# K blocks of six heads issued by ScalarE on its own DMA queue, in a decode step of two attention and two gated layers

## The chip, the cores and the metric

The kernel runs on one core of a Trainium2 chip. The metric is the device time of one execution in microseconds (us). The engines are named as in the profile: PE is TensorE (PEld its weight loads), DVE is VectorE, ACT is ScalarE, POOL is GpSimd and SP is SyncE. SPq and ACTq are the sequencers of SP and ACT, which issue DMA transfers. All transfers run on the 16 DMA engines of the core.

## The reference

One token for each of 4 batch rows goes through attention, a gated block, the same attention again (same weights, same caches) and the same gated block again, each with a residual:

```
x = x + A(layernorm(x));  x = x + B(layernorm(x));  x = x + A(layernorm(x));  x = x + B(layernorm(x))
A:  q = x @ wq                      # 32 query heads of 128, 8 key/value heads, 4 query heads share one
    k, v = the last 2048 of 8192 cached positions of each head
    out = softmax(q k^T / sqrt(128)) v @ wo
B:  (sigmoid(x @ w_gate) * (x @ w_up)) @ w_down      # width 512, inner width 1792
```

All is bf16 in memory. The cached K and V of one batch row and one key/value head are 2048 x 128, 512 KB; there are 32 such blocks of K and 32 of V, 16 MB each.

## The kernel before, in words

**Work and memory.** K of all 8 heads stays in SBUF in `kt` (32 blocks); K is loaded once, transposed in place, and used by both attention layers. V is loaded in both layers. In the first layer its blocks go to `arena`, 77 units of 256 columns, where a block takes 8 units; so 9 blocks fit, and `alloc` (L379) takes the space that was released longest ago. By that rule the second to fourth V block of head n take the place of V blocks of head n-2, the first that of the last block of head n-3. A load into such a place waits for the matmuls that read the old block. `wo` (8 parts of 512 KB in rows of 1 KB) is loaded head by head and stays.

**A head of the first layer**, in the loop at L809, n counting from 0:

- `k_head(n+1)` (L547): the 4 blocks of K of the next head are transposed on PE, 16 transposes a block (L559) in two halves through three PSUM banks, and copied back to `kt` by DVE (L566) and ACT (L570) in turn.
- `scores(n)` (L573): 16 matmuls of q with the transposed K (L583); the maximum on DVE (L592 to L602); the exponential `sexp` on ACT (L605), which writes `pbuf`, the token `("p",)` in the program; four matmuls that turn the probabilities (L614); a copy of them by ACT (L620, `ptc`); the sum and its reciprocal (L627 to L640).
- `load_wo(n)` and four loads of V, then `load_k(n+2)`.
- `pv_wo(n)` (L643): 64 matmuls with V (L656), 16 a block, a scaling on DVE (L666), and 16 matmuls with wo (L675).

All scores of this layer use one PSUM bank, so the scores of head n+1 wait for the exponential of head n.

**What sets the order.** The program lists its operations with what they read and write (`P.op`, L55). `_schedule` (L96) is a planner: it walks a model of the engines with the durations of a table (`_TM`, L259) and takes, on each engine, among the operations that could start within 60 ns of the earliest, the one that is first in the program. This fixes the order on PE, DVE and ACT. DMA transfers are all on SP, apart from the small load of x on ACT (L465), and SP keeps the order of the program: K0, wq, K1, wo0, V0, K2, wo1, V1, K3 and so on (the digit is the head). In the model the transfers go one behind the other through one pipe (L160 to L163). `_assign_sync` (L186) then gives each operation a semaphore and its waits; a DMA on SP gets one of 32 semaphores in turn. An operation given in `order=` comes ahead on the same engine, without a wait on a semaphore.

K of the seventh and eighth head goes to places in `kt` that hold wq at the start (L801 to L806), so those loads also wait for the q projection, which is long over by then.

**Behind the first layer** come the residual, the gated block (`glu`, L708; its weights go to the arena in places that V of the seventh and eighth head leave free), the q projection of the second layer, its V blocks, and the second gated block.

Of the kernel before, what the change touches and what calls it, by code (L numbers as in the profile page):

```python
# [95 lines left out]
def _schedule(ops, tm):  # L96
    for o in ops:
        o.users = []
    for o in ops:
        o.ndeps_left = len(o.deps) + len(o.odeps)  # L100
        for d in o.deps:
            d.users.append(o)
        for d in o.odeps:
            d.users.append(o)
    ready = dict((e, []) for e in ENGINES)
    order = dict((e, []) for e in ENGINES)
    eng_free = dict((e, 0.0) for e in ENGINES)
    sync_all = sorted((o for o in ops if o.eng == "sync"), key=lambda o: (o.prio, o.idx))
    sync_ptr = 0
    for o in ops:  # L110
        if o.ndeps_left == 0:
            ready[o.eng].append(o)
    pipe_free = 0.0
    outstanding = []
    nleft = len(ops)
    tol = tm["pick_tol"]
    sem_lat = tm["sem_lat"]
    while nleft:
        best = None
        best_key = None  # L120
        for e in ENGINES:
            if e == "sync":
                if sync_ptr >= len(sync_all) or sync_all[sync_ptr].ndeps_left:
                    continue
                cand = (sync_all[sync_ptr],)
            else:
                cand = ready[e]
                if not cand:
                    continue
            ef = eng_free[e]  # L130
            tmin = None
            ests = []
            for o in cand:
                t = ef
                for d in o.deps:
                    td = d.finish + sem_lat
                    if td > t:
                        t = td
                ests.append((t, o))
                if tmin is None or t < tmin:  # L140
                    tmin = t
            pick = None
            for x in ests:
                if x[0] <= tmin + tol and (pick is None or x[1].prio < pick[1].prio):
                    pick = x
            key = (pick[0], pick[1].prio)
            if best is None or key < best_key:
                best = pick
                best_key = key
        if best is None:  # L150
            raise RuntimeError("scheduler deadlock")
        t0, o = best
        e = o.eng
        if e == "sync":
            sync_ptr += 1
            if o.dma_bytes:
                if len(outstanding) >= tm["dma_max_out"]:
                    outstanding.sort()
                    t0 = max(t0, outstanding[-tm["dma_max_out"]])
                issue_end = t0 + tm["dma_issue"]  # L160
                xs = max(pipe_free, issue_end + tm["dma_lat0"])
                xe = xs + o.dma_bytes / o.dma_rate
                pipe_free = xe  # L163
                o.start = t0
                o.finish = xe + tm["dma_lat1"]
                outstanding.append(o.finish)
                eng_free[e] = issue_end
            else:
                o.start = t0
                o.finish = t0 + o.dur  # L170
                eng_free[e] = o.finish
        else:
            o.start = t0
            o.finish = t0 + o.dur
            eng_free[e] = o.finish
            ready[e].remove(o)
        order[e].append(o)
        nleft -= 1
        for u in o.users:
            u.ndeps_left -= 1  # L180
            if u.ndeps_left == 0 and u.eng != "sync":
                ready[u.eng].append(u)
    return order


def _assign_sync(ops, order, n_dma_sems):  # L186
    counts = {}
    dma_i = 0
    for e in ENGINES:
        for o in order[e]:  # L190
            if o.sem is not None:
                sem = o.sem
            elif e == "sync":
                sem = ("dma", dma_i % n_dma_sems)
                dma_i += 1
                o.inc = 16
            else:
                sem = ("eng", e)
                o.inc = 1
            o.sem = sem  # L200
            counts[sem] = counts.get(sem, 0) + o.inc
            o.val = counts[sem]
    prev_user = {}
    for o in order["sync"]:
        p = prev_user.get(o.sem)
        if p is not None:
            o.deps.add(p)
        prev_user[o.sem] = o
    snap = {}
    known = dict((e, {}) for e in ENGINES)  # L210
    pos = dict((e, 0) for e in ENGINES)
    done = set()
    total = sum(len(order[e]) for e in ENGINES)
    ndone = 0
    while ndone < total:
        progressed = False
        for e in ENGINES:
            oe = order[e]
            kn = known[e]
            while pos[e] < len(oe):  # L220
                o = oe[pos[e]]
                ok = True
                for d in o.deps:
                    if d.idx not in done:
                        ok = False
                        break
                if not ok:
                    break
                need = {}
                for d in o.deps:  # L230
                    if need.get(d.sem, 0) < d.val:
                        need[d.sem] = d.val
                waits = []
                for s in sorted(need, key=str):
                    v = need[s]
                    if kn.get(s, 0) >= v:
                        continue
                    waits.append((s, v))
                    kn[s] = v
                    ps = snap.get((s, v))  # L240
                    if ps is not None:
                        for s2, v2 in ps.items():
                            if kn.get(s2, 0) < v2:
                                kn[s2] = v2
                o.waits = tuple(waits)
                sn = dict(kn)
                if sn.get(o.sem, 0) < o.val:
                    sn[o.sem] = o.val
                snap[(o.sem, o.val)] = sn
                done.add(o.idx)  # L250
                pos[e] += 1
                ndone += 1
                progressed = True
        if not progressed:
            raise RuntimeError("sync assignment deadlock")
    return counts
# [12 lines left out]
def build(nc, A_x, A_k, A_v, A_wq, A_wo, B_wg, B_wu, B_wd, out):  # L269
    tm = dict(_TM)  # L270
# [40 lines left out]
    def kv_d(cache, b, h):  # L311
        return cache[b, h, SK - W:SK, :].rearrange("(p j) d -> p (j d)", p=128)

    es = contextlib.ExitStack()
    with es:
# [38 lines left out]
        x_sem = es.enter_context(nc.semaphore("x_in"))  # L354
        eng_sems = dict((e, es.enter_context(nc.semaphore("s_" + e))) for e in ENGINES if e != "sync")
        dma_sems = [es.enter_context(nc.semaphore("s_dma%d" % i)) for i in range(N_DMA_SEMS)]

        P = _Plan()

# [50 lines left out]
        def c_act(n):  # L410
            return tm["act_fix"] + n * tm["act_el"]

        def dma(name, dst, src, w, r=(), rate="bw_4k", nbytes=None, sem=None):
            if nbytes is None:
                nbytes = dst.partition_size() * dst.free_nbytes()
            o = P.op("sync", name, 0.0, lambda e, dst=dst, src=src: e.dma_start(dst, src),  # L416
                     r=r, w=w, dma_bytes=nbytes, dma_rate=tm[rate])
            if sem is not None:
                o.sem = sem
                o.inc = 16  # L420
            return o

        def load_block(name, cache, b, h, s):
            dma(name, blk_ap(s), kv_d(cache, b, h), w=blk_tok(s))


        P.op("gpsimd", "ones", 200.0, lambda g: g.memset(ones_f[:], 1.0), w=[("ones_f",)])
# [359 lines left out]
        TBK = [(0, "vector"), (1, "scalar"), (2, "vector"), (0, "scalar"), (1, "vector"), (2, "scalar")]  # L787
        layer_norm(0, math.log(SCALE))

        def load_k(h):  # L790
            for b in range(NB):
                load_block("K_%d_%d" % (h, b), A_k, b, h, kblk(h, b))

        def load_wo(h):
            dma("wo_%d" % h, wo_sb[:, h * WOH:(h + 1) * WOH].rearrange("p (r n) -> p r n", r=REP),
# [13 lines left out]
        for n, h in enumerate(HEADS1):  # L809
            if n + 1 < HKV:  # L810
                k_head(HEADS1[n + 1], TBK)
            scores(0, n, h, 3, MB)
            load_wo(h)
            vs = []
            for b in range(NB):
                s = alloc()
                load_block("V0_%d_%d" % (h, b), A_v, b, h, s)
                vs.append(s)
            if n + 2 < HKV:
                load_k(HEADS1[n + 2])  # L820
            pv_wo(0, n, h, (5, 6), vs)
            for b in range(NB):
                release(vs[b])
# [49 lines left out]
        def sem_h(s):  # L873
            if s[0] == "eng":
                return eng_sems[s[1]]
            if s[0] == "dma":
                return dma_sems[s[1]]
            return x_sem if s[0] == "xin" else out_sem

        def run_engine(eng, name):  # L880
# [49 lines left out]
```

## Time and profile before

| what | value |
|---|---|
| three runs | 190.92, 191.29 and 204.33 us, median 191.29 |
| the profiled execution | 191.58 us, of which the span from first to last instruction is 189.7 us |
| busy | PE 136.0 us (72%), PEld 113.5 (60%), DVE 65.1 (34%), ACT 53.7 (28%), POOL 2.1 (1%) |
| mean granted TensorE clock | 0.684 |
| DMA | 72.48 MB, mean 382 GB/s; 72.10 MB of it on the queue of SP |
| transposes of K on PE (L559) | 47.1 us, 512 of them |
| matmuls with V from the arena (L656) | 23.0 us, idle before them 13.9, of which 13.8 to V's DMA |
| the exponential (L605) | 687 ns each, 16 of them |
| first layer's last V matmuls end | 110.2 us from the start of the span |

Shares are of the span. In the slices of the page, each of the 40 digits stands for 4.74 us and gives tenths of busy time. In lines of the order of time, the columns are the start, the duration, the engine and line, the operation, what it writes and reads, how many were merged, and in brackets the idle time of the engine just before with what ended it. An issue of a transfer is a line of SPq or ACTq; its duration is the issue alone, and the data land later. Idle time of an engine that is not the bottleneck costs nothing.

### The profile page before, as it was taken

What the parts mean: (1) busy time and instruction counts of PE and PEld (TensorE: products, weight loads), DVE (VectorE), ACT (ScalarE), POOL (GpSimd) and SP (SyncE); (2) the same over time, 40 slices, a digit from 0 to 9 for tenths busy, and PEclk for the clock granted to TensorE, in tenths of its full rate; (3) what the DMA queues carried; (4) which work ended last, traced back from release to release, by engine and by line L of the source; (5) the groups of instructions that cost most, each with busy time, mean ns of one, the idle gap of its engine ahead of it and who ended that gap; (6) DMA issues with size and microseconds to landing.
All of it is one profiled execution on the core that took longest, in us unless ns stands there. A gap on an engine that the chain in (4) does not pass through costs nothing.

```text
span 189.7 us, 6050 instructions
## 1 busy us (share of the span) xinstructions
PE 136.0 (72%) x2760; PEld 113.5 (60%) x2760; DVE 65.1 (34%) x204; ACT 53.7 (28%) x91; POOL 2.1 (1%) x10
## 2 busy tenths in 40 slices
PE   2944886979869598795786465364669799985574
PEld 2933764968759397593784354363327466674463
DVE  4410255436345343454244020220067163530220
ACT  2440162554626336263172000000043122220010
POOL 4000000000000000000000000000000000000000
PEclk9996589588797957969579555555597555555555
DMA  6999999999999999999999999999999999999980
GB/s 220 380 416 418 400 403 409 388 411 396 401 406 388 409 399 399 408 390 408 398 397 394 404 406 382 370 355 375 415 413 410 407 407 405 411 409 404 387 272 15
DMA packets 25281, 72.48 MB, mean 382 GB/s; under 512 B 2212, under 2 KB 9896, under 8 KB 24744
## 3 DMA queue, kind: packets, MB, share of 16 engines
q1 hardware_dynamic: 25248, 72.10, 98.2%
q8 instruction: 21, 0.34, 0.7%
q14 instruction: 4, 0.03, 0.0%
q10 hardware_dynamic: 8, 0.00, 0.0%
HBM read 72.09 MB, written 0.00 MB: 380 GB/s over the span
## 4 chain that ended last, share of the span: by engine, by line
DMA 63%; PE 23%; DVE 5%; SPq 4%; ACT 2%; issue 2%; ACTq 0%; DVEq 0%
DMA arena<-in_A_v_cache_dram 33%; DMA kt<-in_A_v_cache_dram 9%; DMA kt<-in_A_k_cache_dram 8%; PE ps L559 6%; DMA arena<-in_B_w_gate_dram 6%; PE ps L583 5%; SPq L416 4%; PE ps L656 4%; DMA arena<-in_B_w_down_dram 4%; DMA arena<-in_A_wq_dram 4%; PE ps L720 2%; ACT pbuf L605 2%; PE ps L675 1%; PE ps L760 1%; PE ps L484 1%
## 5 line engine op out<-in xcount | busy, mean ns | idle before, releaser
L559 PE MATMUL ps<-ident_b,kt 128*128 128x128 bf16 x512 | 47.1, 278 | 0.6 <-DMA kt<-in_A_k_cache_dram 0.3
L559 PEld LDWEIGHTS ps<-ident_b,kt 128*128 128x128 bf16 x512 | 44.9, 131 | 1.3 <-DMA kt<-in_A_k_cache_dram 0.8
L570 ACT COPY kt<-ps 128x1024 bf16<-128x1024 bf16 x32 | 32.2, 1012 | 34.2 <-PE ps L559 33.4
L656 PE MATMUL ps<-pt,arena 128*128 128x4 bf16 x704 | 23.0, 165 | 13.9 <-DMA arena<-in_A_v_cache_dram 13.8
L566 DVE COPY kt<-ps 128x1024 bf16<-128x1024 bf16 x32 | 22.1, 692 | 28.2 <-PE ps L559 28.2
L656 PEld LDWEIGHTS ps<-pt,arena 128*128 128x128 bf16 x704 | 20.4, 99 | 17.8 <-DMA arena<-in_A_v_cache_dram 17.4
L605 ACT ACTIVATE pbuf<-ps,nmg 128x512 bf16<-128x512 f32 x16 | 11.0, 687 | 43.8 <-DVE nmg L602 33.4
L583 PE MATMUL ps<-kt,qs 128*32 128x512 bf16 x256 | 21.2, 466 | 1.8 <-ACT kt L570 1.3
L592 DVE TENSOR_REDUCE nm<-ps 128x1 f32<-128x512 f32 x16 | 10.9, 682 | 17.1 <-PE ps L583 17.1
L656 PE MATMUL ps<-pt,kt 128*128 128x4 bf16 x320 | 10.3, 166 | 4.5 <-issue 3.3
L656 PEld LDWEIGHTS ps<-pt,kt 128*128 128x128 bf16 x320 | 9.5, 104 | 5.3 <-issue 4.0
L583 PEld LDWEIGHTS ps<-kt,qs 128*32 128x32 bf16 x256 | 6.2, 109 | 8.4 <-issue 3.7
L675 PE MATMUL ps<-onb,wo_sb 128*128 128x4 bf16 x256 | 9.2, 167 | 2.8 <-DVE onb L666 2.4
L675 PEld LDWEIGHTS ps<-onb,wo_sb 128*128 128x128 bf16 x256 | 8.3, 104 | 4.1 <-issue 2.6
L620 ACT CAST pt<-ps 128x256 bf16<-128x256 f32 x16 | 6.0, 372 | 14.9 <-PE ps L614 14.9
L666 DVE TENSOR_TENSOR onb<-ps,rz 128x16 bf16<-128x16 f32 x16 | 3.1, 194 | 17.6 <-PE ps L656 17.4
L509 ACT ACTIVATE lnl<-ps 128x4 f32<-128x4 f32 x4 | 0.7, 176 | 29.2 <-PE ps L484 29.2
L614 PEld LDWEIGHTS ps<-ident_b,pbuf 128*128 128x128 bf16 x64 | 3.3, 108 | 8.8 <-ACT pbuf L605 5.7
L614 PE MATMUL ps<-ident_b,pbuf 128*128 128x64 bf16 x64 | 5.4, 215 | 4.2 <-ACT pbuf L605 4.2
L523 PE MATMUL ps<-xn,kt 128*128 128x4 bf16 x128 | 3.9, 166 | 6.1 <-DMA kt<-in_A_wq_dram 6.1
L720 PE MATMUL ps<-xn,arena 128*128 128x4 bf16 x168 | 5.7, 167 | 3.5 <-DMA arena<-in_B_w_up_dram 1.2
L523 PE MATMUL ps<-xn,arena 128*128 128x4 bf16 x128 | 4.7, 167 | 4.9 <-DMA arena<-in_A_wq_dram 4.3
(60 smaller groups left out, 79.2 us busy)
## 6 DMA issues: line engine op xcount, KB each, us to landing
arena<-in_A_v_cache_dram SPq DMA_DIRECT2D x44, 512.0 KB, 12.6
kt<-in_A_k_cache_dram SPq DMA_DIRECT2D x32, 512.0 KB, 13.0
kt<-in_A_v_cache_dram SPq DMA_DIRECT2D x20, 512.0 KB, 13.8
kt<-in_A_wq_dram SPq DMA_DIRECT2D x4, 1024.0 KB, 11.6
wo_sb<-in_A_wo_dram SPq DMA_DIRECT2D x8, 512.0 KB, 14.8
arena<-in_A_wq_dram SPq DMA_DIRECT2D x8, 512.0 KB, 7.0
arena<-in_B_w_gate_dram SPq DMA_DIRECT2D x4, 448.0 KB, 10.5
arena<-in_B_w_up_dram SPq DMA_DIRECT2D x4, 448.0 KB, 10.8
```

The source lines that it names most:

```text
L416: o = P.op("sync", name, 0.0, lambda e, dst=dst, src=src: e.dma_start(dst, src), r=r, w=w, dma_bytes=nbytes, dma_rate=tm[rate])
L523: last = pe.matmul(ps[:, QB, q * NB:(q + 1) * NB], ap[:, (q - q0) * 128:(q - q0 + 1) * 128], xn[:, ktc * NB:(ktc + 1) * NB], start=(st and ...
L559: last = pe.transpose(bankb(bank)[:, jj * 128:(jj + 1) * 128], half[:, jj * 128:(jj + 1) * 128], ident_b[:, :])
L566: lambda v, half=half, bank=bank: v.tensor_copy(half, bankb(bank)[:, 0:1024]),
L570: lambda a, half=half, bank=bank: a.copy(half, bankb(bank)[:, 0:1024]),
L583: last = pe.matmul(ps[32 * b:32 * b + 32, sbk, 0:CB * 128], qs[:, q0:q0 + 32], blk_ap(kblk(h, b))[:, c * CB * 128:(c + 1) * CB * 128], sta ...
L592: lambda v: v.tensor_reduce(nmv, ps[:, sbk, 0:CB * 128], AXX, ALU.max, negate=True),
L605: lambda a: a.activation(pbuf[:, :], ps[:, sbk, 0:CB * 128], ACTF.Exp, bias=gv, scale=1.0, accum_out=zv),
L614: last = pe.matmul(to[:, k], pbuf[:, k * 128:(k + 1) * 128], sel, start=True, stop=True, skip_group_check=True)
L656: last = pe.matmul(ps[:, obk, b * REP:(b + 1) * REP], blk_ap(s)[:, (c * CB + k) * 128:(c * CB + k + 1) * 128], pt[:, w0:w0 + REP], start=( ...
L675: last = pe.matmul(ps[:, WB, c * NB:(c + 1) * NB], wo_sb[:, h * WOH + r_ * D + c * 128: h * WOH + r_ * D + (c + 1) * 128], ov[:, r_ * NB:( ...
L720: last = pe.matmul(ps[:, bank, fc * NB:(fc + 1) * NB], blk_ap(s)[:, fc * 128:(fc + 1) * 128], xn[:, ktc * NB:(ktc + 1) * NB], start=(ktc = ...
```

## The change

`load_k` for the third to eighth head (`n + 2` in the loop, so 24 blocks of 512 KB) is given to ACT's DMA queue in place of SP's. Each head's four issues are ordered behind the last writer of `pbuf` at that place of the program, which is the exponential of head n, two heads in front. This is an order on ACT, not a wait on a semaphore. K of the first two heads stays on SP.

The planner is taught of DMA on other engines: such an issue takes ACT for the table's issue time (450 ns), its data go through the same modelled pipe, and they are not counted in the limit of 16 outstanding transfers that SP has in the model. The second queue gets 32 semaphores of its own.

```
...                                 # _schedule, between the cases of sync and of the compute engines
+        elif o.dma_bytes:
+            issue_end = t0 + tm["dma_issue"]
+            xe = max(pipe_free, issue_end + tm["dma_lat0"]) + o.dma_bytes / o.dma_rate
+            pipe_free = xe
+            o.start = t0
+            o.finish = xe + tm["dma_lat1"]
+            eng_free[e] = issue_end
+            ready[e].remove(o)
...
-            elif e == "sync":
-                sem = ("dma", dma_i % n_dma_sems)
-                dma_i += 1
+            elif o.dma_bytes:
+                sem = ("dma" if e == "sync" else "dmaq", dma_i[e] % n_dma_sems)
+                dma_i[e] += 1
                 o.inc = 16
...
-        def dma(name, dst, src, w, r=(), rate="bw_4k", nbytes=None, sem=None):
+        def dma(name, dst, src, w, r=(), rate="bw_4k", nbytes=None, sem=None, eng="sync", order=()):
...
-            o = P.op("sync", name, 0.0, lambda e, dst=dst, src=src: e.dma_start(dst, src),
-                     r=r, w=w, dma_bytes=nbytes, dma_rate=tm[rate])
+            o = P.op(eng, name, 0.0, lambda e, dst=dst, src=src: e.dma_start(dst, src),
+                     r=r, w=w, dma_bytes=nbytes, dma_rate=tm[rate], order=order)
...
-        def load_k(h):
+        def load_k(h, **kw):
             for b in range(NB):
-                load_block("K_%d_%d" % (h, b), A_k, b, h, kblk(h, b))
+                load_block("K_%d_%d" % (h, b), A_k, b, h, kblk(h, b), **kw)
...
             if n + 2 < HKV:
-                load_k(HEADS1[n + 2])
+                load_k(HEADS1[n + 2], eng="scalar", order=[P.last_w[("p",)]])
             pv_wo(0, n, h, (5, 6), vs)
```

More of the change, by code (lines that the diff above doesn't have):

```diff
@@ L187, in _assign_sync @@
     counts = {}
-    dma_i = 0
+    dma_i = dict((e, 0) for e in ENGINES)
     for e in ENGINES:
@@ L203, in _assign_sync @@
     prev_user = {}
-    for o in order["sync"]:
+    for o in [o for e in ENGINES for o in order[e] if o.dma_bytes]:
         p = prev_user.get(o.sem)
@@ L356, in build @@
         dma_sems = [es.enter_context(nc.semaphore("s_dma%d" % i)) for i in range(N_DMA_SEMS)]
+        dmaq_sems = [es.enter_context(nc.semaphore("s_dmaq%d" % i)) for i in range(N_DMA_SEMS)]
         P = _Plan()
@@ L421, in dma, with load_block @@
             return o
-        def load_block(name, cache, b, h, s):
-            dma(name, blk_ap(s), kv_d(cache, b, h), w=blk_tok(s))
+        def load_block(name, cache, b, h, s, **kw):
+            dma(name, blk_ap(s), kv_d(cache, b, h), w=blk_tok(s), **kw)
         P.op("gpsimd", "ones", 200.0, lambda g: g.memset(ones_f[:], 1.0), w=[("ones_f",)])
@@ L877, in sem_h @@
                 return dma_sems[s[1]]
+            if s[0] == "dmaq":
+                return dmaq_sems[s[1]]
             return x_sem if s[0] == "xin" else out_sem
```

## The prediction

> **What bounds the kernel now.** I read the slices of the span first, then the chain that ended last, then the stretches of the eight heads with their DMA share, and last the order of time on SP, ACT and PE. The slices and the chain, from the profile's page:
>
> ```profile
> DMA  6999999999999999999999999999999999999980
> GB/s 220 380 416 418 400 403 409 388 411 396 401 406 388 409 399 399 408 390 408 398 397 394 404 406 382 370 355 375 415 413 410 407 407 405 411 409 404 387 272 15
> ...
> DMA 63%; PE 23%; DVE 5%; SPq 4%; ACT 2%; issue 2%; ACTq 0%; DVEq 0%
> ...
> arena<-in_A_v_cache_dram SPq DMA_DIRECT2D x44, 512.0 KB, 12.6
> kt<-in_A_k_cache_dram SPq DMA_DIRECT2D x32, 512.0 KB, 13.0
> ```
>
> All 16 DMA engines are at 90% or more from the second slice to the last but two, and the chain is mostly DMA. A K block lands a median 13.0 us after its issue, though 0.524 MB at 401 GB/s last 1.3 us: some ten transfers are always queued. Two stretches of the first attention layer, columns PE, PEld, DVE, ACT and POOL busy, granted clock, DMA share, GB/s:
>
> ```profile
> 52.00:64.00 12.00, 9.52 (x174) 8.05 (x166) 4.89 (x12) 5.20 (x7) 0.00 (x0) 0.86 1.03 400
> 64.00:76.00 12.00, 10.07 (x170) 9.14 (x166) 4.92 (x12) 5.20 (x7) 0.00 (x0) 0.72 1.04 401
> ```
>
> The DMA share is 1.03 and over (packets overlap a little), so the engines never rest. A head moves 9 transfers (4 K, 4 V, one wo), 4.72 MB, which at 401 GB/s take **11.8 us**; that is the period of the heads. PE is busy 9.5 to 10.1 of 12 us, so it is close behind. A change of who issues the transfers moves the end only if it leaves the DMA engines without work, or makes a head's chain of compute longer than 11.8 us.
>
> **The change part by part.** The issues on SP and the exponentials on ACT, in order of time:
>
> ```profile
> 19.15 3.94 SPq L416 DMA_DIRECT2D kt<-in_A_k_cache_dram  x4
> 32.46 2.26 SPq L416 DMA_DIRECT2D kt<-in_A_k_cache_dram  x4
> 55.51 2.51 SPq L416 DMA_DIRECT2D kt<-in_A_k_cache_dram  x4
> ...
> 29.39 0.69 ACT L605 ACTIVATE pbuf<-ps,nmg 128x512 bf16<-128x512 f32 x1 [1.50 <-DVE nmg L602]
> 33.31 0.69 ACT L605 ACTIVATE pbuf<-ps,nmg 128x512 bf16<-128x512 f32 x1 [2.39 <-PE ps L656]
> 54.01 0.69 ACT L605 ACTIVATE pbuf<-ps,nmg 128x512 bf16<-128x512 f32 x1 [2.69 <-PE ps L656]
> ```
>
> *Removed from SP*: 24 issues at a median 434 ns, 10.4 us of a queue that mostly stands with its ring full (the first V issue, at 8.20 us, lasted 8.15 us). Worth nothing by itself. SP then runs ahead with wo and V until the arena's slots stop it (V of head n, second block on, needs the slots of head n-2).
>
> *Added to ACT*: 4 issues a head, from 0.434 us (SP's row) to 0.56 us (ACT's one issue, x, at 0.81 us): 1.7 to 2.2 us behind each of six exponentials. I take 1.8. Behind them on ACT wait the copy of the transposed probabilities (L620), for which PV waits, and the copies of the next transposes (L570). In the fourth head the exponential ends at 54.78 us and the first such copy starts at 57.75: 2.97 us, less 0.37 for L620, is 2.6 us of cover. Cost **0**; without the cover it would be 1.8 us a head, 11 us in all.
>
> *Moved in time*: if the exponentials stayed where they are, the third head's K would be issued at 30.2 instead of 19.15 us, the fourth's at 34.1 instead of 32.46, the sixth's at 54.8 instead of 55.51, and the others within 0.7 us of now. So only the third head's K is really late, by 11 us. How long K then takes no row shows, since nothing now shares the engines with a second queue. Bounds: 2.10 MB alone at 401 GB/s, 5.2 us; the slowest transfer of now, 19.2 us from issue to landing. I take 10 to 13 us, next to the row of 13.0.
>
> The Trainium skill, "DMA: Bandwidth & Descriptors", section "Queues, rings and completion order", says that each DMA engine takes turns between its queues packet by packet; K would then have half the rate, an estimate of 10.5 us for four blocks, inside what I take. No trace of before shows it. Its section "Issuing engines are not separate DMA queues" speaks against the change: issuing from several engines saves only issue time. The 10.4 us above, off the critical path, agree.
>
> So the third head's K is there at 42 to 45 us, its transposes end at 44 to 46 instead of 40.0, and everything behind them is **4 to 6 us late**. Is that kept, lost or repaid? A head as PE runs it now:
>
> ```profile
> 55.12 0.28 PE L614 MATMUL ps<-ident_b,pbuf 128*128 128x64 bf16 x4
> 55.64 0.54 PE L675 MATMUL ps<-onb,wo_sb 128*128 128x4 bf16 x16 [0.24 <-DVE onb L666]
> 56.04 5.62 PE L559 MATMUL ps<-ident_b,kt 128*128 128x128 bf16 x64
> 61.50 0.20 PE L635 MATMUL ps<-zd,ones_b 128*128 128x16 bf16 x2
> 62.59 0.55 PE L656 MATMUL ps<-pt,arena 128*128 128x4 bf16 x16 [0.90 <-DMA arena<-in_A_v_cache_dram]
> 63.08 1.05 PE L583 MATMUL ps<-kt,qs 128*32 128x512 bf16 x16
> ```
>
> The planner takes, of what is ready within 60 ns, the operation that is earliest in the program, and it believes that K queues behind all that SP has issued. Working its rule by hand (for the order, not for a time), I get per head: transposes of n+1, PV of n whole, scores of n+1, softmax, transposes of n+2. Now PV straddles the scores. The chain of a head would be 5.62 (transposes) + 1.74 (PV, the row at 42.12 us) + 1.05 (scores) + 1.57 (end of scores at 64.13 to exponential at 65.70) + 0.78 (exponential) + 0.28 (L614) = **11.0 us**, against 11.8 us of DMA. The lateness shrinks by some 0.7 us a head and is 2 to 4 us at the last. K of head n+2 is wanted, last block, about 16 us behind the exponential of n (11 + 0.4 + 4.2), so 10 to 13 us are in time. The engines starve only if V's slots and K both run out; SP has by the slots always 6 to 8 us of transfers issued ahead. The end of the layer now:
>
> ```profile
> 103.59 0.28 PE L614 MATMUL ps<-ident_b,pbuf 128*128 128x64 bf16 x4
> ...
> 109.57 0.59 PE L656 MATMUL ps<-pt,arena 128*128 128x4 bf16 x16 [0.67 <-DMA arena<-in_A_v_cache_dram]
> ```
>
> The last head's probabilities are copied at 104.27 us and its last V block comes at 109.5; the three blocks before need 1.3 us, so softmax may be 3.9 us late for nothing. What is over falls on the gated block, whose matmuls wait for weights from 115.35 to 118.81 us: another 3 us. With 2 to 4 us late, I charge **0.4 us** for the two places where the engines could run short (the K wait of the third head, the first weight issue at 102.35 us, which waits for PV of the seventh head).
>
> **Sum**: SP 0, ACT 0, lateness 0.4. The profiled execution took 191.58 us (span 189.7, 1.9 around it), 0.3 above the median of the three runs, 191.29. Forecast **192.0 us**, its own range 190.3 to 194.2. A measurement of this kernel tells about 2% (3.8 us) from no change.
>
> **The rivals.**
> 1. *K comes last and the lead of two heads is lost (slower).* Now K of a head lands two heads before its V. If the ACT queue's K lands over 16 us behind its exponential, because SP's backlog of V goes first, every head waits for K, and the eighth head's K lands with the last V. Then behind the last landing stand transposes of a block (1.4), its copy (1.1), scores 1.05, softmax 2.35, L614 0.28, copy 0.45 and PV 1.74 = 8.4 us, where now one block's 0.6 stands; less the 3 us that the gated block absorbs, +4.8: **196.4 us** (194 to 198). For it: 19.2 us occurs now. Against: K's own queue is then short. 21%.
> 2. *ACT stands in the issue.* SP's K issues reach 2.45 us when the ring is full. If ACT's last 1.3 us each (the pace of landing), 5.2 us a head stand before the copies against 2.6 of cover: 2.6 x 6 heads = 15.6, less 3.9 and 3 of slack: +8.7, **200.3 us**. Against: ACT has at most 8 blocks out, and SP got 13 transfers out before its ring stopped it. 9%.
> 3. *Two queues move more bytes.* If the rate of the heads (401) rose to that of the slices at 10 to 19 us (417), the 80 us from 30 to 110 shrink by 3.1: **188.5 us**, 1.6% faster. Against: the lower rate goes with wo's short rows, which stay. 8%, half of it over 2%.
> 4. *The order is all that the change sets*: the issues may be planned behind other ACT work, later than the exponential. By 2 to 6 us, this leads into rival 1 and is counted there.
>
> **How the numbers follow.** Forecast 60%, rival 1 21%, rival 2 9%, rival 3 8%, an unnamed loss 2%. Slower by over 2% (above 195.4): most of rival 1 (17), rival 2 (9), 3 of the forecast, 2 unnamed = 31%. Faster by over 2%: 5%. Within: 64%. The range from 188.8 to 198.0 holds the forecast, most of rival 1 and half of rival 3, and leaves out rival 2.
>
> **What would show it.** Right: DMA share 1.0 and about 400 GB/s in every stretch from 10 to 110 us; ACT's issues near 0.45 us each; exponentials of heads four to eight 2 to 6 us later than now; last V block at 109 to 111 us; transposes from the fifth head on not waiting for K. Rival 1: idle time of the transposes put down to K's DMA, and PV without waits for V. Rival 2: ACT issues above 1 us and copies waiting behind them. Rival 3: over 410 GB/s in the heads. What makes me wrong most easily: the order that the planner writes, which I have only by hand, and the share of the engines that the second queue gets.

## The result, and the profile after

The changed kernel takes 192.68 us (median of 20 runs, 191.07 to 194.79) against 191.42 us of the kernel before (20 runs): a ratio of **1.0053, 95% interval 1.0033 to 1.0073**, 1.0 us slower. The ratio leaves out slow runs, those over 1.5% above the fastest of their kernel (one of 20 on either side), so it isn't quite that of the two medians. The forecast was 192.0 us with no change clear of 2%, and its range holds the time. In the experiments below, on two different chips, the same kernel came to 1.0012 (0.9978 to 1.0046) and 1.0040 (1.0009 to 1.0071).

The page of the changed kernel, its slices and its chain:

```profile
DMA  5999999999999999999999999999999999999980
GB/s 206 425 427 411 393 402 390 403 399 402 405 389 403 396 404 400 398 409 393 406 402 393 354 363 399 365 405 411 407 408 411 406 408 403 412 407 405 391 285 16
...
PE 44%; DMA 25%; SPq 13%; DVE 8%; ACT 6%; issue 3%; ACTq 0%; DVEq 0%
...
arena<-in_A_v_cache_dram SPq DMA_DIRECT2D x44, 512.0 KB, 15.5
kt<-in_A_k_cache_dram ACTq DMA_DIRECT2D x24, 512.0 KB, 10.6
```

Two stretches of the heads, and the one where the first layer ends:

```profile
52.00:64.00 12.00, 8.49 (x166) 7.58 (x166) 4.93 (x13) 5.10 (x7) 0.00 (x0) 0.86 1.04 397
64.00:76.00 12.00, 8.41 (x166) 7.46 (x166) 6.16 (x16) 5.20 (x7) 0.00 (x0) 0.85 1.03 400
100.00:110.00 10.00, 7.99 (x156) 7.08 (x154) 4.66 (x12) 4.80 (x7) 0.00 (x0) 0.84 0.99 373
```

The rate in the heads is what it was (397 and 400 GB/s, before 400 and 401), and K on ACT's queue lands a median 10.6 us behind its issue. But the chain has changed hands: mostly PE where it was mostly DMA. The stretch from 100 to 110 us moved 399 GB/s before and moves 373 now. The mean granted clock, 0.664 against 0.684, is not what makes the difference: beside e9 the kernel before took 190.8 to 191.5 us in executions at 0.663 and 190.9 to 191.7 us at 0.685.

This profiled execution, 191.07 us, is the fastest of the 20, so it shows the mechanism but not the whole loss. A second look at the same kernel (e9 below, span 191.7 us, 2.0 us over the profile of before) has the same shape with a larger hole.

Where the time begins to be lost, in the order of time on PE from the second to the fourth head, changed kernel:

```profile
34.91 0.57 PE L665 MATMUL ps<-pt,arena 128*128 128x4 bf16 x16
37.10 0.59 PE L665 MATMUL ps<-pt,arena 128*128 128x4 bf16 x16 [1.63 <-DMA arena<-in_A_v_cache_dram]
39.67 0.59 PE L665 MATMUL ps<-pt,arena 128*128 128x4 bf16 x16 [1.97 <-DMA arena<-in_A_v_cache_dram]
42.22 0.58 PE L665 MATMUL ps<-pt,arena 128*128 128x4 bf16 x16 [1.96 <-DMA arena<-in_A_v_cache_dram]
43.18 0.57 PE L684 MATMUL ps<-onb,wo_sb 128*128 128x4 bf16 x16 [0.38 <-DVE onb L675]
43.61 6.05 PE L568 MATMUL ps<-ident_b,kt 128*128 128x128 bf16 x64
50.78 1.05 PE L592 MATMUL ps<-kt,qs 128*32 128x512 bf16 x16 [1.12 <-ACT kt L579]
```

The same stretch in the kernel before (L559 are the transposes, L656 PV):

```profile
33.14 1.01 PE L559 MATMUL ps<-ident_b,kt 128*128 128x128 bf16 x8
...
34.42 5.55 PE L559 MATMUL ps<-ident_b,kt 128*128 128x128 bf16 x56
...
42.12 1.74 PE L656 MATMUL ps<-pt,arena 128*128 128x4 bf16 x64
```

In the changed kernel the four blocks of V of the second head (L665) arrive 2.56 us apart, 205 of the 402 GB/s, beside K of the third and fourth head on the other queue. The transposes of the third head (L568) stand behind them in PE's order and start at 43.6 us; in the kernel before they stood in front of that PV and started at 33.1.

Starts of the eight exponentials of the first layer, from the order of time on ACT (us):

| kernel | 1 | 2 | 3 | 4 | 5 | 6 | 7 | 8 |
|---|---|---|---|---|---|---|---|---|
| before | 29.4 | 33.3 | 44.0 | 54.0 | 65.7 | 77.9 | 89.2 | 102.3 |
| changed | 29.2 | 33.1 | 53.4 | 65.5 | 76.2 | 87.7 | 98.2 | 108.8 |
| late by | -0.2 | -0.2 | 9.5 | 11.5 | 10.5 | 9.8 | 9.0 | 6.5 |

From the fourth to the eighth head the changed kernel takes 10.8 us a head, the kernel before 12.1. It catches up 5 of 11.5 us, not all. What is left meets the first gate weight, which waits for PV of the seventh head to leave its place. The queue of SP, first the changed kernel, then its second look (e9):

```profile
105.86 0.33 SPq L425 DMA_DIRECT2D arena<-in_B_w_gate_dram  x1
```

```profile
108.18 0.33 SPq L425 DMA_DIRECT2D arena<-in_B_w_gate_dram  x1
```

Before, this issue came at 102.35 us. SP's last V issue ends at 96.3 us (changed) and 98.1 us (e9), SP then issues nothing for ten us, and the engines run dry. In stretches, the kernel before and then e9:

```profile
100.00:110.00 10.00, 5.26 (x150) 4.13 (x138) 2.25 (x8) 1.15 (x3) 0.00 (x0) 0.70 1.04 399
110.00:118.00 8.00, 4.95 (x125) 4.48 (x122) 1.15 (x7) 0.38 (x2) 0.00 (x0) 0.50 1.04 395
```

```profile
100.00:110.00 10.00, 8.57 (x166) 7.83 (x166) 4.45 (x12) 5.10 (x7) 0.00 (x0) 0.83 0.84 314
110.00:118.00 8.00, 4.30 (x107) 3.96 (x107) 2.79 (x14) 1.15 (x3) 0.00 (x0) 0.67 0.97 358
```

At 399 GB/s the missing bytes of e9 are worth 10 x (399 - 314)/399 = 2.1 us and 8 x (395 - 358)/395 = 0.7 us. A part comes back: from 126 to 135 us e9 moves 409 GB/s and the kernel before only 374, 0.8 us. The net, 2.0 us, is the difference of the two spans. In the fastest execution the same sums are 0.7 + 0.2 - 0.7, and it ends even with before. Both kernels move the same bytes, so such a sum tells where the time goes, not why.

### The profile page after: what moved, and what is told of

Read it like the earlier page. It is cut to its first block, busy times and chain, and to the rows that moved or that the text cites. A ratio compares the mean times of both kernels' runs of the same rounds, so it can differ in the third digit from the quotient of the medians.

```text
span 189.3 us, 6057 instructions
## 1 busy us (share of the span) xinstructions
PE 133.5 (70%) x2760; PEld 110.5 (58%) x2760; DVE 65.7 (35%) x204; ACT 53.5 (28%) x91; POOL 2.1 (1%) x10
## 4 chain that ended last, share of the span: by engine, by line
PE 44%; DMA 25%; SPq 13%; DVE 8%; ACT 6%; issue 3%; ACTq 0%; DVEq 0%
PE ps L568 17%; SPq L425 13%; DMA kt<-in_A_v_cache_dram 9%; DMA arena<-in_A_v_cache_dram 9%; PE ps L592 8%; PE ps L665 8%; DMA arena<-in_A_wq_dram 4%; DMA arena<-in_B_w_down_dram 3%; PE ps L729 3%; ACT pbuf L614 3%; DVE nm L601 3%; ACT kt L579 2%; PE ps L623 2%; PE ps L493 2%; PE ps L684 2%
## 5 line engine op out<-in xcount | busy, mean ns | idle before, releaser
L568 PE MATMUL ps<-ident_b,kt 128*128 128x128 bf16 x512 | 44.6, 268 | 0.9 <-DMA kt<-in_A_k_cache_dram 0.5
L568 PEld LDWEIGHTS ps<-ident_b,kt 128*128 128x128 bf16 x512 | 42.6, 125 | 1.6 <-issue 0.7
L665 PE MATMUL ps<-pt,arena 128*128 128x4 bf16 x704 | 21.2, 165 | 5.8 <-DMA arena<-in_A_v_cache_dram 5.8
L592 PE MATMUL ps<-kt,qs 128*32 128x512 bf16 x256 | 23.4, 505 | 2.6 <-ACT kt L579 2.2
L665 PEld LDWEIGHTS ps<-pt,arena 128*128 128x128 bf16 x704 | 19.9, 101 | 6.2 <-DMA arena<-in_A_v_cache_dram 6.2
L665 PEld LDWEIGHTS ps<-pt,kt 128*128 128x128 bf16 x320 | 9.5, 104 | 4.2 <-issue 3.4
L665 PE MATMUL ps<-pt,kt 128*128 128x4 bf16 x320 | 10.3, 166 | 2.2 <-issue 1.5
L532 PE MATMUL ps<-xn,arena 128*128 128x4 bf16 x128 | 4.7, 167 | 4.4 <-DMA arena<-in_A_wq_dram 3.8
L532 PEld LDWEIGHTS ps<-xn,kt 128*128 128x128 bf16 x128 | 3.6, 100 | 6.8 <-DMA kt<-in_A_wq_dram 6.8
## 6 DMA issues: line engine op xcount, KB each, us to landing
kt<-in_A_k_cache_dram ACTq DMA_DIRECT2D x24, 512.0 KB, 10.6
kt<-in_A_wq_dram SPq DMA_DIRECT2D x4, 1024.0 KB, 11.5
```

Source lines behind the costliest of these rows:

```text
L532: last = pe.matmul(ps[:, QB, q * NB:(q + 1) * NB], ap[:, (q - q0) * 128:(q - q0 + 1) * 128], xn[:, ktc * NB:(ktc + 1) * NB], start=(st and ...
L568: last = pe.transpose(bankb(bank)[:, jj * 128:(jj + 1) * 128], half[:, jj * 128:(jj + 1) * 128], ident_b[:, :])
L592: last = pe.matmul(ps[32 * b:32 * b + 32, sbk, 0:CB * 128], qs[:, q0:q0 + 32], blk_ap(kblk(h, b))[:, c * CB * 128:(c + 1) * CB * 128], sta ...
L665: last = pe.matmul(ps[:, obk, b * REP:(b + 1) * REP], blk_ap(s)[:, (c * CB + k) * 128:(c * CB + k + 1) * 128], pt[:, w0:w0 + REP], start=( ...
```

## The experiments

Four questions had to be told apart: is it the late K of the third head, the second queue itself, ACT's issues, or the order that the planner writes once it reckons with the late K?

### e1: the changed kernel once more

No edit. 

> The changed kernel once more, for a second trace. Theory A (the third head starts late, the heads behind it run at the pace of PE, and the DMA engines run short of work where the first gate weight waits for PV of the seventh head): 1.003 to 1.008 of the kernel before; exponential of the third head near 53 us, last PV of the first layer ends at 112 to 114 us against 110.2, and DMA share below 1.0 somewhere between 104 and 112 us. Rival B (the two queues or ACT's issues cost something everywhere): the same time, but a rate below 395 GB/s already between 40 and 100 us, or copies on ACT waiting behind issues.

Measured 1.0012 (0.9978 to 1.0046); exponential of the third head at 53.4 us, DMA share 0.79 from 106 to 108 us, and 402, 404, 397, 400 GB/s in the stretches from 30 to 76 us. Theory A's place is right; rival B's low rate is not there. The ratio is below the 1.003 that theory A asked for, and the size could not be told from nothing on this chip.

### e2: K of the third head stays on SP

```
+                if n == 0:
+                    load_k(HEADS1[n + 2])
+                else:
                     load_k(HEADS1[n + 2], eng="scalar", order=[P.last_w[("p",)]])
```

> K of the third head stays on SP, 20 of the 24 moved blocks stay on ACT. Theory A (all of the loss begins with the late third head): exponential of the third head back near 44 us, last PV of the first layer ends at 110 to 111 us, ratio 0.998 to 1.002. Rival B (second queue and ACT's issues cost by themselves): 5/6 of the loss stays, ratio 1.004 to 1.006.

Measured **1.0437 (1.0386 to 1.0487)**, 199.9 to 203.5 us. Both theories missed. The trace is of the longest of its seven executions. In it the third exponential is back at 44.7 us, but the fourth stands at 73.1. PE of e2 shows why:

```profile
49.77 0.59 PE L665 MATMUL ps<-pt,arena 128*128 128x4 bf16 x16 [2.02 <-DMA arena<-in_A_v_cache_dram]
...
55.10 0.58 PE L665 MATMUL ps<-pt,arena 128*128 128x4 bf16 x16 [2.88 <-DMA arena<-in_A_v_cache_dram]
57.02 0.58 PE L665 MATMUL ps<-pt,arena 128*128 128x4 bf16 x16 [1.33 <-DMA arena<-in_A_v_cache_dram]
59.57 0.59 PE L665 MATMUL ps<-pt,arena 128*128 128x4 bf16 x16 [1.96 <-DMA arena<-in_A_v_cache_dram]
61.52 0.59 PE L665 MATMUL ps<-pt,arena 128*128 128x4 bf16 x16 [1.37 <-DMA arena<-in_A_v_cache_dram]
...
62.91 6.44 PE L568 MATMUL ps<-ident_b,kt 128*128 128x128 bf16 x64
```

The planner had put PV of the second and of the third head ahead of the transposes of the fourth. In its model K queues behind all V that SP has issued, so it believes that K comes last. On the chip the queues share, K is early and V is late, and PE waits for V with K lying ready. Later DMA runs dry: 327 GB/s from 100 to 112 us and 167 from 112 to 124, worth 12 x (73 + 233)/400 = 9.2 us at 400 GB/s, of the 12.0 us by which this span is longer than that of before (201.7 against 189.7). This pointed to the order on PE, which the next runs hold fixed.

### e3: the old order, all 24 loads on ACT

The planner sees K on SP as before; its order for PE, DVE and SP is kept, and only then the K loads are taken from SP's list and put behind the same exponentials on ACT.

```
-                load_k(HEADS1[n + 2], eng="scalar", order=[P.last_w[("p",)]])
+                k0 = len(P.ops)
+                load_k(HEADS1[n + 2])
+                moved.append((P.last_w[("p",)], P.ops[k0:]))
...                                 # behind _schedule: gate is the exponential of head n, ks the K loads of head n + 2
+        for gate, ks in moved:
+            la = order["scalar"]
+            i = la.index(gate) + 1
+            for j, o in enumerate(ks):
+                order["sync"].remove(o)
+                o.eng = "scalar"
+                if j == 1 and la[i].name.startswith("ptc"):
+                    i += 1
+                la.insert(i, o)
+                i += 1
```

> The order on PE, DVE and SP is the one planned for the kernel before; only the 24 K loads are taken out of SP's order and put behind the same exponentials on ACT. Theory A1 (the lateness of 9.5 us comes from the new order on PE, which puts PV of the second head, fed at half rate, ahead of the transposes of the third): exponential of the third head at 46 to 49 us, last PV of the first layer ends at 110 to 111 us, ratio 0.998 to 1.003. Rival A2 (the late issue of K alone makes the lateness): exponential of the third head at 51 to 54 us, ratio 1.004 to 1.007.

Measured 0.9969 (0.9935 to 1.0002), third exponential at 48.9 us, last PV of the layer to 111.0 us. PE of e3 at the transposes of the third head:

```profile
36.05 1.03 PE L568 MATMUL ps<-ident_b,kt 128*128 128x128 bf16 x8 [2.49 <-DMA kt<-in_A_k_cache_dram]
...
39.96 4.96 PE L568 MATMUL ps<-ident_b,kt 128*128 128x128 bf16 x48 [1.59 <-DMA kt<-in_A_k_cache_dram]
```

So with the old order the late K costs 4.9 us at the third head, and no time is lost at the end: theory A1. But the hole at the first gate weight is here as well:

```profile
106.49 0.33 SPq L425 DMA_DIRECT2D arena<-in_B_w_gate_dram  x1
```

This issue comes later than in the changed kernel (105.86 us), and from 106 to 108 us e3 moves 237 GB/s where e1 moves 257. A hole by itself is therefore not a loss; e9 to e11 below take this up.

### e4: another gate weight first

```
-            for ktc in range(NC):
-                for nm, bank in (("g", GB), ("u", UB)):
+            for ktc, nm in [(2, "g")] + [(k, m) for k in range(NC) for m in "gu" if (k, m) != (2, "g")]:
+                for bank in ((GB if nm == "g" else UB),):
...
```

> In the gated block the third gate weight is loaded and used first; its place in the arena was V of the sixth head, so its load needs not wait for PV of the seventh. Theory A (the shortage of transfers near 106 us is the loss): 0.46 MB more are at hand there, worth up to 1.1 us; 304 GB/s near 106 us become 380 or more, ratio 0.999 to 1.003. Rival C (the loss is the later end of the compute chain, and transfers are not short for long): ratio stays at 1.004 to 1.007.

Measured 0.9994 (0.9958 to 1.003), beside 1.0012 of e1 on the same chip. From 106 to 108 us it moved 340 GB/s where e1 moved 257, short of the 380 of theory A, and its own stretch from 126 to 135 us fell to 366. The intervals overlap, so this is inconclusive: with one transfer more at hand the hole was narrower in this trace, and whether that is worth time is open.

### e5: the old order, third head's K on SP

e3 with the four loads of the third head left on SP (`if n > 0:` ahead of `moved.append`).

> As e2 (K of the third head on SP, the other 20 moved blocks behind the same exponentials on ACT), but PE, DVE and SP keep the order planned for the kernel before. Theory A1 (the 4.4% of e2 came from the order on PE, which put PV of the second and third head, fed at half rate, ahead of the transposes of the fourth): exponential of the fourth head at 54 to 58 us instead of 73, ratio 0.993 to 1.002. Rival B (K on two queues starves V whatever the order): exponential of the fourth head behind 65 us, ratio over 1.03.

Measured 0.9952 (0.9916 to 0.9989); the fourth exponential at 59.9 us, 2 us behind what A1 expected, and 13 us ahead of e2. The loads of this kernel stand on the same queues behind the same exponentials as in e2. The order of work accounts for the 4.4%; rival B falls.

### e6: twice the issues on ACT

The changed kernel with each K load issued as two halves on the same semaphore; the planned order is the same.

```
-            o = P.op(eng, name, 0.0, lambda e, dst=dst, src=src: e.dma_start(dst, src),
+            def e_dma(e, dst=dst, src=src):
...
+                e.dma_start(dst[:, 0:1024], src[:, 0:1024]).then_inc(sem_h(o.sem), 16)
+                return e.dma_start(dst[:, 1024:2048], src[:, 1024:2048])
+            o = P.op(eng, name, 0.0, e_dma,
...
```

> The changed kernel, same planned order on every engine, but each of the 24 K loads on ACT is issued as two halves: 8 issues behind each exponential instead of 4, 1.3 to 1.7 us more on ACT for a head. Theory D (ACT's cover is used up: in the trace of the changed kernel the first copy of a transposed half follows the last K issue by 0.05 to 0.4 us, and the heads run at the pace of PE): 1 to 1.5 us a head from the fourth on, eighth exponential at 112 to 116 us instead of 108.8, ratio 1.015 to 1.03. Rival E (three PSUM banks and DVE take it up): eighth exponential at 109 to 110 us, ratio 1.000 to 1.008.

Measured 1.0362 (1.0307 to 1.0418), the eighth exponential at 116.1 us: theory D, and more than it asked. ACT and PE of e6 in one head:

```profile
80.94 0.45 ACTq L429 DMA_DIRECT2D kt<-in_A_k_cache_dram  x1
81.44 1.93 ACT L584 COPY kt<-ps 128x1024 bf16<-128x1024 bf16 x2 [2.83 <-PE ps L573]
```

```profile
78.04 2.93 PE L573 MATMUL ps<-ident_b,kt 128*128 128x128 bf16 x32
82.60 1.87 PE L573 MATMUL ps<-ident_b,kt 128*128 128x128 bf16 x16 [1.62 <-ACT kt L584]
```

The first copies start 0.05 us behind the last issue, and the transposes stand 1.62 us for them (0.94 and 0.80 in the two neighbouring heads). In the changed kernel the first copy follows the last issue by 0.40, 0.22 and 0.05 us behind the exponentials of the fourth, fifth and sixth head, and there it waits for PE, not for ACT: its four issues just fit. The last of the three:

```profile
88.87 1.30 ACTq L425 DMA_DIRECT2D kt<-in_A_k_cache_dram  x3
90.22 1.01 ACT L579 COPY kt<-ps 128x1024 bf16<-128x1024 bf16 x1 [0.98 <-PE ps L568]
```

With the halves, in rows of 2 KB, the rate in the heads is also lower, 391 GB/s instead of 400 with the engines as busy (DMA share 1.05), so the 3.6% isn't all ACT's.

### e7: K one head later, in the old order

e3 with the gate one head on (`moved.append(("sexp0_%d" % HEADS1[n + 1], P.ops[k0:]))`).

> The order planned for the kernel before on PE, DVE and SP; the K loads stand on ACT one head later, behind the exponential of the head just in front. Theory (K is wanted about 16 us behind the exponential two heads in front; one head later it can't be in time): each head then waits for K, a period of 1.3 (issues) + 8 to 10.6 (landing) + 1.4 (last transposes) + 1.1 + 1.05 + 1.57 + 0.78 = 15 to 18 us for six heads against 11.8; less 7 us of slack 12 to 30 us, ratio 1.06 to 1.16. Rival (K lands as soon as asked, since V's slots run out): period 12 to 13 us, ratio 1.00 to 1.03.

Measured 1.1672 (1.1585 to 1.176), 222.9 to 226.7 us. The exponentials of the third to eighth head are 15.2 to 18.2 us apart, as worked out; the ratio is just above the range given. The waits and the whole stretch, e7:

```profile
PE ps L568 <- DMA kt<-in_A_k_cache_dram: 36.1, 15, 7.1
```

```profile
60.00:135.00 75.00, 43.32 (x725) 37.36 (x726) 21.46 (x52) 23.19 (x31) 0.00 (x0) 0.69 0.76 275
```

This is rival 1 at full strength: transposes wait 36.1 us for K, SP waits 97.7 us in all for PV (L665) to leave V's places (58.6 in the changed kernel), and the engines move 275 GB/s. Of the two gates tried, only the one two heads in front serves.

### e8: the new order, all K on SP

The planner's result for the changed kernel, with the K loads then put back to SP at their old places.

```
+        for o in [o for o in order["scalar"] if o.dma_bytes]:
+            order["scalar"].remove(o)
+            o.eng = "sync"
+            order["sync"].append(o)
+        order["sync"].sort(key=lambda o: o.idx)
```

> The order on PE, DVE and ACT is the one planned for the changed kernel, but all K loads are on SP, in SP's order of before: the new order without the second queue. Theory A1 (half of the lateness is the order): PV of the second head, ahead of the transposes of the third, waits for V that stands behind K on SP; transposes start at 38 to 41 us instead of 33, third exponential at 47 to 51 us (before 43.95, changed kernel 53.4), ratio 1.000 to 1.005. Rival A2 (only the late issue counts): third exponential at 44 to 45 us, ratio 0.998 to 1.001.

Measured **1.0090 (1.0056 to 1.0125)**: the order by itself, with no second queue and no late issue, is slower. Its PE from the second head on:

```profile
39.36 0.59 PE L665 MATMUL ps<-pt,arena 128*128 128x4 bf16 x16 [3.91 <-DMA arena<-in_A_v_cache_dram]
40.64 0.59 PE L665 MATMUL ps<-pt,arena 128*128 128x4 bf16 x16 [0.69 <-DMA arena<-in_A_v_cache_dram]
41.92 0.59 PE L665 MATMUL ps<-pt,arena 128*128 128x4 bf16 x16 [0.69 <-DMA arena<-in_A_v_cache_dram]
43.20 0.59 PE L665 MATMUL ps<-pt,arena 128*128 128x4 bf16 x16 [0.70 <-DMA arena<-in_A_v_cache_dram]
44.17 0.57 PE L684 MATMUL ps<-onb,wo_sb 128*128 128x4 bf16 x16 [0.38 <-DVE onb L675]
44.60 6.35 PE L568 MATMUL ps<-ident_b,kt 128*128 128x128 bf16 x64
```

With one queue the V blocks come 1.28 us apart (2.56 in the changed kernel), but behind K, and the transposes, whose K is there, stand behind PV all the same. The third exponential is at 54.7 us, later than the 47 to 51 of A1 and even than in the changed kernel.

### e9 to e11: the changed kernel beside the two best, on one chip

e9, the changed kernel: 

> The changed kernel beside the next two on one chip, since its loss was 0.5% on one chip and 0.1% on another. Theory (new order costs 0.9%, second queue gives 0.3 to 0.5% back): 1.002 to 1.007, above both of the next two.

e10, as e5: 

> As e5: order of before, K of the third head on SP, the other 20 blocks on ACT. Theory: 0.993 to 0.999 again, a small gain over both kernels. Rival: the gain of e5 was chance, 0.999 to 1.002.

e11, as e3: 

> As e3: order of before, all 24 blocks on ACT. Theory: 0.994 to 1.000 again, 0.3 to 0.8% below the changed kernel. Rival: no difference from the changed kernel beyond 0.2%.

| kernel | ratio to before | interval |
|---|---|---|
| e9: changed | 1.0040 | 1.0009 to 1.0071 |
| e10: old order, third head's K on SP | 0.9982 | 0.9947 to 1.0016 |
| e11: old order, all 24 on ACT | 0.9990 | 0.9960 to 1.0020 |

The changed kernel is above before again and, by the middle values, 0.5 to 0.6% above both kernels with the old order; both their intervals just overlap its own. Set run against run, over the runs that those ratios rest on, e9 is the longer in 85% of the pairs with e10 and 89% of those with e11, and e1 in 84% of those with e3 on its chip. e11 and e3 differ from the changed kernel in the planned order alone, so the order costs it about half a percent. The gain of e5 was not seen again clear of no change: e5 and e10 both lie below 1, but only e5 with its whole interval. No version is shown to beat the kernel before.

Why the hole costs time in some kernels and not in others can be read from the traces together. Each row is one execution; e4 is left out, since it loads another weight first.

| trace | first gate weight issued, us | GB/s, 100 to 110 us | GB/s, 126 to 135 us | span, us |
|---|---|---|---|---|
| before | 102.35 | 399 | 374 | 189.7 |
| e11 | 104.92 | 391 | 372 | 189.8 |
| e10 | 105.33 | 386 | 391 | 189.3 |
| changed | 105.86 | 373 | 407 | 189.3 |
| e1 | 106.12 | 364 | 405 | 189.5 |
| e5 | 106.33 | 368 | 405 | 189.9 |
| e3 | 106.49 | 354 | 406 | 189.9 |
| e8 | 107.35 | 330 | 408 | 191.9 |
| e9 | 108.18 | 314 | 409 | 191.7 |
| e6 | 112.46 | 340 | 370 | 197.0 |
| e2 | 116.89 | 381 | 377 | 201.7 |
| e7 | 138.45 | 218 | 275 | 222.8 |

Up to 106.5 us, 4 us later than before, the span doesn't move; from 107.4 us on it is longer, and each us of the issue is then worth about one of the span. The changed kernel lies on both sides of that edge (105.86, 106.12 and 108.18 us), which fits a loss of 1 us on average with some executions that lose nothing. This is a pattern over kernels that differ in more than this one issue; no run moved the issue alone.

## Why the prediction was right

That 192.0 us came so close to 192.7 is in part luck. PE fell behind by twice as much as was priced, made up more per head than was priced, and what was left met enough slack at the end. Two of the signs named for a right prediction did not come: the exponentials of heads four to eight are 6.5 to 11.5 us late instead of 2 to 6, and from 100 to 110 us the engines move 373 GB/s instead of about 400.

**The bound.** Right. The engines keep 400 GB/s through the heads whichever queue K is on. That rules out rivals 2 and 3: ACT's issues took 0.33 to 0.51 us, none stood for a full ring, and the rate did not rise (397 to 402 GB/s). But the chain of the changed kernel is 44% PE: from the third head on PE, not DMA, set the pace.

**SP, 0.** Right as far as shown: SP was emptied of K and nothing was won. That SP mostly stood for a full ring was read one-sidedly: in the kernel before, from 8 to 100 us, 29.0 us of its waits are put down to PV (L656), which leaves V's places.

**ACT, 0.** Right, but the cover was read too wide. The 2.6 us came from the old order, where PV stands between exponential and transposes. In the new order the transposes follow at once from the fourth head on, the copies start 0.05 to 0.4 us behind the last issue, and e6, with twice the issues, pays.

**K's time to land, 10 to 13 us.** Right where the sum needed it: the third head's last K block lands 12.3 us behind its issue, at 43.5 us (forecast 42 to 45). The last blocks of the later heads take 17.0, 11.9, 11.4, 12.0 and 13.6 us, and the median of all blocks is 10.6. The Trainium skill, "DMA: Bandwidth & Descriptors", section "Queues, rings and completion order", has each engine take turns between queues packet by packet. The estimate of 10.5 us from it was for four blocks at half rate, so that it comes near the median of single blocks is chance. The turns themselves are in the trace: from 35 to 37 us SP's queue moved 114 packets and 0.41 MB, ACT's 110 and 0.39; from 41 to 43 us 165 and 166 packets, but 0.18 and 0.61 MB. So K has half of the bytes while SP's packets are as large as its own, and three quarters when most of SP's packets are under 2 KB, as wo's rows of 1 KB are.

**Late by 4 to 6 us.** This step failed; it measured 9.5 us at the third head and 11.5 at the fourth. I worked out the planner's order for the later heads (transposes, PV, scores, rightly) and not where it changes first: PV of the second head, fed at half rate, ahead of the third head's transposes. e3 shows 4.9 us when the order is kept, and e8 shows more than 9.5 with the new order and no late K. So the late issue was priced rightly and the order was not. Nor is the half rate needed for it: in e8, with K on SP, the last of these V blocks is used at 43.2 us, in the changed kernel at 42.2.

**A chain of 11.0 us a head against 11.8.** About right: 10.5 to 11.6 us in the changed kernel. The kernel before took 12.1 there, so 1.25 us a head were made good rather than 0.7, and 6.5 us were left at the last head instead of 2 to 4. Heads shorter than the 11.8 us of DMA were possible because the engines had gone on at 402 GB/s while PE stood (30 to 52 us), so the loads were ahead.

**3.9 us of slack at the layer's end.** Right: 6.5 us late, and the last PV ends at 112.3 against 110.2 us, 2.1 late; 2.6 was to be expected.

**0.4 us where the engines run short.** The place was right, the first gate weight behind PV of the seventh head (102.35 us before, 105.9 to 108.2 now). The size was not: 1.0 us by the ratio, from a net of about 0 in the fastest execution to 2.0 us in e9. In the table above nothing is lost while that issue is up to 4 us late, so with the priced lateness of 2 to 4 us the term would have been about nothing; this is the same error met again.

**Rival 1** did not come true as I had it, K last. e7 shows that it exists and what it costs, 32 us by the ratio, if K is one head later. I had priced it at 4.8 us, by its last head alone; every head pays. e2 shows its mirror image: V last, where the order expects K last.

## What to carry to other kernels

Where a planner writes the order from a model, a change of the model is two changes: the one that was meant and a new order on every engine. Price both, and run the old order with the new queue and the new order with the old queue before the queue is blamed or praised. Here the second queue took its share from the first at once (V blocks 2.56 us apart instead of 1.28), so work that waits for the first must not stand in front of work that is ready.

## What had not been expected

- Leaving the latest of the moved loads where it was, which looked like a pure repair, cost 4.4% (e2), only by the order that the planner then wrote.
- By the middle values the new order is slower without the second queue (1.0090) than with it (1.0012 to 1.0053 in three measurements). These are of different chips, and only e1's interval lies clear of e8's, so this is not settled.
- A late end of the first layer is partly given back: before, the stretch from 126 to 135 us moves 374 GB/s, in the changed kernel 407 and in e9 409. e11, which moves 391 GB/s from 100 to 110 us, falls to 372 there as well. That the two shortages stand in for each other was seen in most traces, but not in e4, which has both, and was not tested by itself.
